# Seven block products in place of eight in part of a fused attention and feed-forward kernel

## The chip, the cores and the metric

The kernel runs on one core of a Trainium2 chip. Its engines are named as the profile names them: PE (TensorE, matmuls; its weight loads are PEld), DVE (VectorE), ACT (ScalarE), POOL (GpSimd) and SP (SyncE, which here only issues DMAs). The metric is the device time in microseconds, as the median of several runs; lower is better.

## The reference

A linear attention makes `x`, and a multiplicative feed-forward is applied to it:

```
q_s = exp(q - max_d(q));  q_s /= sum_d(q_s) + 1e-9          # q, k, v: 8 batches x 8 heads x 576 x 64, float32
k_s = exp(k - max_s(k));  k_s /= sum_s(k_s) + 1e-9
x   = q_s @ (k_s^T @ v)          # per batch and head; laid out as 4608 tokens x 512
h   = (x @ w1) * (x @ w2) @ w3   # w1, w2: 512 x 1024;  w3: 1024 x 1024
out = h @ w_out                  # w_out: 1024 x 512;  out: 4608 x 512, float32
```

## The kernel before

`w3 @ w_out` is multiplied out first (`fold`, lines 337 to 350: transposes `w3t`, their copies `w3T`, products `pf`, and the scaled copy `W3O`, kept in 16 bits). What is left per token group is two "up" products, `x @ w1` and `x @ w2`, their product `ab`, and one "down" product `ab @ W3O`.

There are nine token groups `c`. Groups 0 to 7 hold 512 tokens of one batch each; group 8 (`xtail`) holds the 64 tokens per batch that are left over. `attention(b)` makes the group's `x`: column maxima of k (`kmx`, `cb`), subtraction and exponential (`ksub`, `kexp`), a 16-bit copy of v (`vc`), the small products `kv`, and for q the row maximum, subtraction, exponential, sum and normalisation (`qmx`, `qsub`, `qexp`, `qsm`, `qeps`, `qrc`, `qn`), a transposing DMA (`qd`), and the products `xm` and `xt` with their copies `xs` and `xts`, which write `x`.

`chunk(c)` holds the feed-forward of a group. The 1024 hidden columns are worked in slices of 128 (lines 716 to 748). For one slice `up(…, 1)` accumulates four matmuls (the 512 inputs in blocks of 128) of `x @ w2` over 512 tokens in one PSUM bank; `bs` copies that bank to SBUF in 16 bits; `up(…, 0)` does the same with `w1`; `ab` multiplies the second bank by the copy (line 741, always on DVE). Groups 0 and 1 are cut into two halves of 256 tokens, so that their matmuls have 256 columns; all others have 512. `down(tb)` accumulates eight matmuls of 512 output columns for 128 tokens; `os` copies the bank and `store` sends it off from SP. In group 8 the last block of 128 tokens is cut into three parts (`down2`, `os2`, `tail`).

All work is put into a `Plan` as steps with an engine, their inputs (`needs`) and what they take and give back: PSUM banks (`ps`, eight), output buffers (`osb`, six), the 16-bit copies (`bsb`, six). A text, `ORDER`, lists the steps one by one. A letter after a slash chooses the engine where there is a choice (A for ACT, D for DVE, P for POOL). Each engine works through its own steps in just this order, and waits only for the inputs and buffers of the step that is next. Steps marked `port` that lie on POOL and DVE are linked in `run`: where two of them follow each other on different engines, the later one waits for the earlier one. Steps on ACT, and DVE steps without the mark (`ab`, `bs`, `os`, reductions), are not linked.

## Time and profile before

| what | value |
|---|---|
| median of 3 runs | 235.95 us (235.83 to 236.02) |
| profiled execution, span from the first to the last instruction | 234.6 us |
| granted PE clock | 1.000 |
| PE busy | 228.0 us, 1938 matmuls |
| DVE busy | 185.7 us, 310 instructions |
| ACT busy | 112.8 us, 178 instructions |
| POOL busy | 115.7 us, 77 instructions |
| DMA | 46.84 MB, mean 200 GB/s |

The profile gives the profiled execution's span; the runs are some 1.35 us longer than that, for what lies before the first and behind the last instruction. In rows of groups, a line holds the source line, the engine, the operation, output and inputs with their shapes, the count, then busy time in us and the mean duration of one in ns, then the idle time of the engine just before, and what ended it. In rows of a time line or of the chain of waits the first number is the start in us from the start of the span, the second the length in us. "128x512" is 128 partitions of 512 elements.

### The profile page before, as it was taken

How to read it: one execution, taken by the hardware profiler on the slowest of the kernel's cores; microseconds unless marked ns; L12 is line 12 of the kernel's file. 1: busy time of each engine (PE TensorE's matmuls, PEld its weight loads, DVE VectorE, ACT ScalarE, POOL GpSimd, SP SyncE). 2: the span in 40 equal slices, each digit the busy share in tenths (PEclk: the TensorE clock that was granted, in tenths of full speed). 3: DMA queues.
4: the chain of work that ended last, by engine and by line, in shares of the span. 5: the costliest groups of instructions: out<-in, count | busy, mean ns of one | idle time of the engine just before them, and what ended most of it. 6: DMA issues, size and time to landing. Idle time of an engine off the chain costs nothing.

```text
span 234.6 us, 4828 instructions
## 1 busy us (share of the span) xinstructions
PE 228.0 (97%) x1938; PEld 119.6 (51%) x1938; DVE 185.7 (79%) x310; ACT 112.8 (48%) x178; POOL 115.7 (49%) x77
## 2 busy tenths in 40 slices
PE   7898999999999999999999999999999999999995
PEld 2454568856876445444444444444544444444443
DVE  3989779989999999999899979979686247634642
ACT  2646763686737876675885265344504210000101
POOL 8244410788969399799938983790700000000000
DMA  6999999999999996999499997453391016005035
GB/s 221 215 293 224 305 243 243 389 274 276 273 298 334 398 373 187 252 402 332 42 218 396 268 236 229 91 25 79 70 183 30 0 36 145 0 6 129 3 75 193
DMA packets 38358, 46.84 MB, mean 200 GB/s; under 512 B 18368, under 2 KB 21824, under 8 KB 38336
## 3 DMA queue, kind: packets, MB, share of 16 engines
q1 hardware_dynamic: 32464, 35.92, 55.6%
q0 software_dynamic: 5728, 10.55, 19.2%
q8 instruction: 15, 0.25, 0.4%
q10 hardware_dynamic: 144, 0.07, 0.1%
q14 instruction: 7, 0.06, 0.1%
HBM read 38.80 MB, written 9.44 MB: 206 GB/s over the span
## 4 chain that ended last, share of the span: by engine, by line
PE 89%; DMA 9%; POOL 1%; issue 0%; ACT 0%; POOLq 0%
PE pab L726 53%; PE po L748 24%; DMA w<-in_moe_w_dram 9%; PE pf L347 3%; PE po L763 3%; PE pkv L443 2%; PE xm L582 2%; PE w3t L337 1%; PE xt L582 1%; POOL w L305 0%; PE pkv L452 0%; POOL ident masks.py:199 0%; ACT osb L223 0%; POOL ident masks.py:197 0%; POOLq masks.py:199 0%
## 5 line engine op out<-in xcount | busy, mean ns | idle before, releaser
L726 PE MATMUL pab<-x,w2sb 128*128 128x512 f16 (+1 forms) x320 | 64.9, 337 | 0.0
L726 PE MATMUL pab<-x,w1sb 128*128 128x512 f16 (+1 forms) x320 | 64.9, 337 | 0.0
L741 DVE TENSOR_TENSOR ab<-pab,bsb 128x512 f16<-128x512 f32 x72 | 47.7, 682 | 16.8 <-PE pab L726 15.2
L748 PE MATMUL po<-W3O,ab 128*128 128x512 f16 x256 | 58.4, 379 | 0.0
L223 ACT CAST bsb<-pab 128x512 f16<-128x512 f32 x49 | 28.0, 584 | 49.5 <-PE pab L726 49.3
L726 PEld LDWEIGHTS <-w1sb 128*128 128x128 f16 x352 | 34.3, 98 | 27.7
L726 PEld LDWEIGHTS <-w2sb 128*128 128x128 f16 x352 | 34.1, 98 | 28.1 <-issue 0.2
L417 POOL TENSOR_TENSOR k<-k,cb 128x1152 f32<-128x1152 f32 x13 | 34.0, 2628 | 19.2 <-DVE q L486 10.3
L748 PEld LDWEIGHTS <-ab 128*128 128x128 f16 x256 | 24.4, 98 | 30.0 <-issue 2.3
L530 POOL TENSOR_TENSOR en<-eq,qr 128x1024 f16<-128x1024 f16 (+1 forms) x14 | 29.6, 2125 | 16.7 <-ACT qr L518 10.5
L378 DVE TENSOR_REDUCE km<-k 128x128 f32<-128x1152 f32 x14 | 30.3, 2167 | 0.0
L223 ACT COPY osb<-po 128x512 f32<-128x512 f32 (+2 forms) x26 | 14.7, 564 | 28.7 <-PE po L748 17.6
L486 POOL TENSOR_TENSOR q<-q,qm 128x1280 f32<-128x1280 f32 (+1 forms) x13 | 27.8, 2144 | 0.9 <-DVE qm L480 0.9
L480 DVE TENSOR_REDUCE qm<-q 128x16 f32<-128x1024 f32 (+2 forms) x16 | 21.2, 1331 | 3.8 <-DMA q<-in_q_dram 3.8
L494 ACT ACTIVATE eq<-q 128x1024 f16<-128x1024 f32 (+2 forms) x16 | 18.7, 1169 | 9.4 <-DVE q L486 8.5
L512 DVE TENSOR_REDUCE qr<-eq 128x16 f32<-128x1024 f16 (+2 forms) x16 | 21.3, 1340 | 0.2 <-ACT eq L494 0.2
L425 ACT ACTIVATE ek<-k 128x1152 f16<-128x1152 f32 x16 | 18.1, 1161 | 6.2 <-POOL k L417 6.2
L223 DVE CAST bsb<-pab 128x512 f16<-128x512 f32 x23 | 15.8, 687 | 6.4 <-PE pab L726 6.1
L227 ACT ACTIVATE x<-xm 128x512 f16<-128x512 f32 x27 | 14.4, 600 | 12.5 <-PE xm L582 12.5
L347 PE MATMUL pf<-wosb,w3T 128*128 128x512 f16 x64 | 15.6, 379 | 0.4 <-DMA wosb<-in_moe_w_out_dram 0.4
L223 DVE COPY osb<-po 128x512 f32<-128x512 f32 (+1 forms) x12 | 7.8, 654 | 9.0 <-PE po L748 4.6
L223 ACT COPY w3T<-w3t 128x1024 f16<-128x1024 f16 x8 | 8.1, 1011 | 5.3 <-PE w3t L337 4.1
(64 smaller groups left out, 175.4 us busy)
## 6 DMA issues: line engine op xcount, KB each, us to landing
out_dram<-osb SPq DMA_DIRECT2D x65, 128.0 KB, 3.1
q<-in_q_dram SPq DMA_DIRECT2D x6, 1152.0 KB, 8.4
k<-in_k_dram SPq DMA_DIRECT2D x6, 1152.0 KB, 6.9
v<-in_v_dram SPq DMA_DIRECT2D x6, 1152.0 KB, 8.7
w<-in_moe_w_dram POOLq DMA_DIRECT2D x8, 256.0 KB, 11.6
q<-in_q_dram SPq DMA_DIRECT2D x2, 576.0 KB, 4.3
k<-in_k_dram POOLq DMA_DIRECT2D x2, 576.0 KB, 13.4
k<-in_k_dram POOLq DMA_DIRECT2D x1, 1152.0 KB, 14.4
```

The costliest lines, as they stand in the source:

```text
L223: return [(nc.scalar.copy if eng == "ACT" else engine[eng].tensor_copy)(out=out, in_=in_)]
L347: nc.tensor.matmul(st["pf", ft], lhsT=st["w3T", ft][:, gt, :], rhs=wosb[:, gt, :], start=(gt == 0), stop=(gt == N_FT - 1))
L378: dve.tensor_reduce(out=st["km", b][:, two(hp), :], in_=kb[:, two(hp), :, :].rearrange("p h j d -> p h d j"), axis=AX.X, op=ALU.max)
L417: return [engine[eng].tensor_tensor(out=kb[:, two(hp), :, :], in0=kb[:, two(hp), :, :], in1=st["cb", b][:, two(hp), None, :].broadcast_to( ...
L480: dve.tensor_reduce(out=st["qm", b][:, hs, j], in_=qb[:, hs, j, :], axis=AX.X, op=ALU.max, **({"negate": True} if (b, p) in FEXP else {}))
L486: return [engine[eng].tensor_tensor(out=qb[:, hs, j, :], in0=qb[:, hs, j, :], in1=st["qm", b][:, hs, j, None].broadcast_to([P, nh, n, D]), ...
L494: nc.scalar.activation(out=st["eq", b, p], in_=qb[:, hs, j, :], func=AF.Exp)
L512: dve.tensor_reduce(out=st["qr", b][(slice(None), *part(p))], in_=st["eq", b, p], axis=AX.X, op=ALU.add)
L530: return [engine[eng].tensor_tensor(out=st["en", b][:, j, hs, :].rearrange("p j h d -> p h j d"), in0=st["eq", b, p], in1=st["qr", b][:, h ...
L726: nc.tensor.matmul(st["p", one, c, sub, u][:, a * (t1 - t0):(a + 1) * (t1 - t0)], lhsT=w[:, ct, fb * P:(fb + 1) * P], rhs=x()[:, ct, t0:t1 ...
L741: dve.tensor_tensor(out=st["ab", c][:, nf * u:nf * u + nf, t0:t1], in0=cut(st["p", 0, c, sub, u]), in1=cut(st["bsb", c, sub, u]), op=ALU.mult)
L748: nc.tensor.matmul(st["po", c, tb], lhsT=st["ab", c][:, ft, tb * P:(tb + 1) * P], rhs=W3O[:, ft, :], start=(ft == 0), stop=(ft == N_FT - 1))
```

## The change

In the last three groups (`SU`: 6, 7 and 8) the up products, and in groups 5, 6 and 7 (`SD`) the down products, are computed as 2 x 2 blocks by Winograd's form of Strassen's algorithm: seven block products, with sums and differences of blocks before and after, in place of eight.

For the up products the blocks of one factor are the upper and lower half (of the 512 inputs) of `w1` and of `w2`; those of the other are the two halves of the inputs and the two halves of 256 tokens of `x`. The result's four blocks are `x @ w1` and `x @ w2` for the two token halves. One set of seven products is made for each `g`, a slice of 256 hidden columns, of which a group has four. A block product `um` is four matmuls of 256 columns (two slices of 128 hidden columns, two blocks of 128 inputs) into one bank. Products 1, 6, 5 and 3 follow each other in the same bank A, each added to what is there; products 7 and 4 share bank B; product 2 has bank C. Between them copies `ue` leave the banks as float32 into eight scratch slots (`sc`, the parts of the first input buffers of q and v): of 1, of 1+6, of 1+6+5, and of 7. Sums `uc` then give `x @ w1` of the first half (1: DVE, from bank C), `x @ w2` of the first half (3: DVE, from bank B) and of the second half (4: POOL or DVE, from two scratch slots). `ab` of the first half is a product of two SBUF operands (POOL or DVE), that of the second half reads bank A (DVE).

Sums ahead of the products: `ws`, eight steps of 1024 elements once, for `w1` and `w2` (seven on POOL, one on DVE, in the place of `w316`), and `xd`, four steps of 512 elements for each of the three groups (eight on DVE, four on POOL). For the down products `wt` makes four differences of `W3O` blocks once (1024 elements, all on POOL), `ad` four sums of `ab` blocks per group (1024 elements, nine on DVE, three on POOL); `dm` is a block product of eight matmuls of 256 columns, in banks A, B and C as above, with copies `de`, sums `dc` and two stores of twice 256 KB per group in place of four of 256 KB.

Counted over the whole: 48 `up` steps with 24 `bs` and 24 `ab`, and 12 `down` steps with 12 `os`, become 84 `um`, 48 `ue`, 36 `uc`, 24 `ab`, 12 `xd`, 8 `ws`, 21 `dm`, 12 `de`, 12 `dc`, 12 `ad` and 4 `wt`. PSUM keeps eight banks and there are still six output buffers, now in one tile (`outs`); the transposed `w3T` and a buffer of `kmx` move into the tile `aux` that `wt` later writes.

`ORDER` is the same up to the second group's third up product (`up.1.1.0.2`), and written anew from there on. The weight sums lie on POOL between `qsub.2.1` and `ksub.7.0`, except `ws.4.1`, on DVE in the last stage. Four `vc` steps more are on ACT instead of POOL. Of the 48 `bs` steps that remain 44 are on ACT and 4 on DVE (before: 49 and 23); of the `os` steps 22 are on ACT and 4 on DVE (before: 26 and 12). The attention of the last group ends later, among the block products, and the stores `st.0.0` and `st.0.1` leave after the group 4 products have begun.

The diff, cut; the part of `ORDER` that is shown runs from the end of group 5's up products to the last store:

```diff
--- before.py
+++ after.py
...
+    def own(self, ring, aps):
+        self.slots[ring] = list(aps)
+
+    def grab(self, s):
+        free = self.slots[s["takes"]]
+        got = [free.pop(0) for _ in range(s["slots"])]
+        self.held[s["name"]] = sorted(k for k, _ in got), got[0][1], s["takes"]
+
+    def free(self, name):
+        ks, _, ring = self.held.pop(name)
+        self.slots[ring] += [(k, self.full[ring][k]) for k in ks]
...
+ksub.7.1/P qd.6.0 xm.6.0 qsm.7.1 xm.6.1 xs.6.1.1/A xt.5 xts.5.1/D st.4.0 down.4.2 xs.6.0.0/A st.4.1 xs.6.0.1/D
+xd.6.1/P um.6.0.1 os.4.2/D xs.6.1.0/A xd.6.2/D xt.6 xts.6.1/A um.6.1.1 ue.6.1.1/A up.1.5.0.7 um.6.1.2 xts.6.0/D
+ue.6.0.1/D st.3.3 um.6.0.6 vc.7.0/A ab.5.0.6 bs.5.0.7/A xd.6.3/D um.6.1.6 ue.6.1.2/A xts.5.0/A um.6.0.7 ad.5.3/D
+qeps.7.1/A ue.6.0.7/A qsm.7.0 um.6.1.7 up.0.5.0.7 xd.6.4/D uc.6.1.1 dm.5.1 ue.6.0.2/D ue.6.1.7/A qrc.7.1 qeps.7.0/A
+qrc.7.0 kexp.7.1 ab.5.0.7 down.4.3 ad.5.1/D ad.5.2/D de.5.1/A um.6.1.4 uc.6.1.3 os.4.3/A um.6.0.2 qn.7.1/P um.6.0.4
+uc.6.0.3 um.6.0.5 um.6.2.1 uc.6.0.1 ue.6.0.4/D uc.6.0.4/D st.3.2 um.6.2.7 um.6.3.1 dm.5.2 ue.6.3.1/A ws.4.1/D qn.7.0/D
+ue.6.2.1/A um.6.2.2 st.3.0 dc.5.1 uc.6.2.1 um.6.1.5 dm.5.6 ue.6.1.4/A um.6.0.3 ab.6.0.1 de.5.2/A uc.6.1.4/P um.6.3.6
+qd.7.0 um.6.2.6 um.6.1.3 ab.6.1.1 dm.5.7 de.5.7/D ue.6.2.7/A um.6.2.4 qd.7.1 dm.5.5 ue.6.2.2/A uc.6.2.3 ad.5.4/P
+kexp.7.0 ab.6.1.0/P kv.7 kv2.7 dm.5.4 ue.6.3.2/A um.6.3.5 um.6.2.5 xm.7.0 xm.7.1 ab.6.2.0/P de.5.4/A dc.5.3 xs.7.0.1/D
+xs.7.1.1/D st.4.2 dc.5.4/P ue.6.2.4/A uc.6.2.4/D xs.7.0.0/A xd.7.1/D xs.7.1.0/A xd.7.3/D dm.5.3 dc.5.2/A um.6.3.2
+uc.6.3.1 xd.7.2/D xt.7 xts.7.1/A st.5.1 um.6.3.7 ue.6.3.7/A ue.6.3.4/A um.7.0.1 ue.7.0.1/A ab.6.0.0/D ad.6.3/D
+um.6.2.3 um.7.2.1 xts.7.0/D ab.6.2.1 st.5.0 xd.8.1/D um.7.1.1 ue.7.1.1/A um.7.0.7 xd.7.4/D ue.7.0.7/A um.7.0.6
+ue.7.0.2/A um.6.3.4 uc.6.3.3 um.6.3.3 uc.6.3.4/P um.7.1.7 ue.7.1.7/D um.7.0.5 um.7.0.4 ue.7.0.4/A uc.7.0.4/P ab.6.3.1
+dm.6.7 uc.7.0.3 um.7.0.2 ue.7.2.1/A uc.7.0.1 ab.7.0.0/P um.7.0.3 ab.7.0.1 um.7.1.6 ue.7.1.2/A um.7.1.4 uc.7.1.3 dm.6.1
+de.6.1/A um.7.1.5 ue.7.1.4/A ad.6.1/D ad.6.2/D ab.6.3.0/D ad.6.4/D um.7.2.7 um.7.1.2 uc.7.1.1 uc.7.1.4/P um.7.3.2
+um.7.3.1 ue.7.3.1/A uc.7.3.1 dm.6.6 de.6.2/A um.7.2.6 um.7.3.6 ue.7.2.2/A xd.8.3/P ue.7.2.7/A ue.7.3.2/A dm.6.2 dc.6.1
+um.7.2.2 uc.7.2.1 um.7.2.5 ue.7.2.4/A um.7.2.4 uc.7.2.3 um.7.3.7 ue.7.3.7/D um.8.0.1 um.7.1.3 ab.7.1.0/P xd.8.2/P
+de.6.7/A ab.7.1.1 uc.7.2.4/D dm.6.4 um.7.3.4 um.7.2.3 uc.7.3.3 dm.6.5 de.6.4/A um.8.0.2 xd.8.4/P dc.6.3 ab.7.2.0/D
+dc.6.4/P ue.8.0.1/D uc.8.0.1 ab.7.3.0/D um.8.0.7 ue.8.0.7/A um.7.3.5 ue.7.3.4/D uc.7.3.4/P um.8.1.1 ue.8.1.1/A dm.6.3
+um.8.1.7 ue.8.1.7/A ad.7.3/P um.8.1.6 um.8.2.1 ue.8.1.2/A ab.7.2.1 ue.8.2.1/A um.7.3.3 ab.7.3.1 um.8.1.4 um.8.1.2
+uc.8.1.3 st.4.3 um.8.1.5 um.8.0.6 ue.8.1.4/D uc.8.1.4/P ue.8.0.2/A um.8.2.6 uc.8.1.1 ab.8.1.0/P dc.6.2/D st.6.0
+um.8.0.4 ue.8.2.2/A um.8.2.2 uc.8.2.1 um.8.3.1 um.8.0.5 ue.8.0.4/A uc.8.0.4/P dm.7.1 um.8.3.7 de.7.1/A uc.8.0.3
+ab.8.0.0/P um.8.2.7 um.8.2.5 ue.8.3.1/D um.8.3.6 um.8.3.2 ue.8.3.7/D ue.8.2.4/A ue.8.3.2/D um.8.3.4 uc.8.3.3 um.8.2.3
+um.8.3.5 uc.8.3.1 um.8.0.3 ad.7.1/P ad.7.2/D ue.8.2.7/A um.8.2.4 st.6.1 uc.8.2.3 dm.7.7 de.7.7/D ab.8.2.0/D dm.7.6
+dm.7.2 dc.7.1 dm.7.4 uc.8.2.4/D ab.8.2.1 ab.8.3.0/D de.7.2/A dc.7.3 dm.7.5 down.8.0 os.8.0/A st.8.0 de.7.4/D
+ue.8.3.4/A um.8.1.3 ab.8.1.1 dc.7.4/P ab.8.0.1 uc.8.3.4/D down.8.1 os.8.1/A st.7.1 st.8.1 ad.7.4/D um.8.3.3 ab.8.3.1
+down.8.2 os.8.2/A st.8.2 dm.7.3 down.8.3.0 down.8.3.256 dc.7.2/A os.8.3.256/D down.8.3 st.7.0 os.8.3.0/D st.8.3.256
+st.8.3.0 os.8.3/A st.8.3
...
+    SU = [6, 7, 8]
+    SD = [5, 6, 7]
+    flat = lambda t: t.rearrange("p h j d -> p (h j d)")
+    auxf = flat(aux)
+    w3Tbuf = [auxf[:, i * 1024:(i + 1) * 1024].rearrange("p (r c) -> p r c", r=N_FT) for i in range(2)]
+    kmtbuf = auxf.bitcast(F32)[:, 1024:2048].rearrange("p (h j d) -> p h j d", h=HH, j=4)
+    wsum = w316.rearrange("p (s k) f -> p s k f", s=4)
+    turn = lambda c, cs: (c - min(cs, default=0)) % 2
+    adbuf = [flat(t).bitcast(F16)[:, 0:4096].rearrange("p (s f t) -> p s f t", s=4, f=4) for t in inbuf["k"]]
+    xdbuf = [t.rearrange("p a j i d -> p (a j i d)")[:, 0:2048].rearrange("p (s k t) -> p s k t", s=4, k=2)
+             for t in v16buf]
+    plan.own("osb", [(i, outs[:, i, :]) for i in range(6)])
+    spare = [flat(inbuf[n][i])[:, 512 * x:512 * x + 512] for i in range(1) for n in "qv" for x in range(4)]
+    plan.own("sc", list(enumerate(spare)))
+    plan.own("w3T", list(enumerate(w3Tbuf)))
...
+        def xd(i, eng):
+            X, xv = xdbuf[turn(c, SU)], x()
+            lo, hi = slice(0, 256), slice(256, 512)
+            a, b = {1: (xv[:, 0:2, hi], xv[:, 0:2, lo]), 2: (xv[:, 2:4, hi], X[:, 0]),
+                    3: (xv[:, 2:4, hi], xv[:, 0:2, hi]), 4: (xv[:, 2:4, lo], X[:, 1])}[i]
+            return minus(eng, X[:, i - 1], a, b)
+
+        BANK = {1: "A", 6: "A", 5: "A", 3: "A", 7: "B", 4: "B", 2: "C"}
+
+        def um(g, p):
+            X, xv = xdbuf[turn(c, SU)], x()
+            lo, hi = slice(0, 256), slice(256, 512)
+            w, k0, r = {1: (w1sb, 0, xv[:, 0:2, lo]), 2: (w1sb, 2, xv[:, 2:4, lo]), 3: (wsum[:, 3], 0, xv[:, 2:4, hi]),
+                        4: (w2sb, 2, X[:, 3]), 5: (wsum[:, 0], 0, X[:, 0]), 6: (wsum[:, 1], 0, X[:, 1]),
+                        7: (wsum[:, 2], 0, X[:, 2])}[p]
+            t = bank2(("u" + BANK[p], c, g))
+            for u in range(2):
+                fb = 2 * g + u
+                for kk in range(2):
+                    nc.tensor.matmul(t[:, u, :], lhsT=w[:, k0 + kk, fb * P:(fb + 1) * P], rhs=r[:, kk, :],
+                                     start=(p in (1, 2, 7) and u == 0 and kk == 0), stop=(u == 1 and kk == 1),
+                                     skip_group_check=True)
+
+        def slot(name):
+            return plan.held[name][1].rearrange("p (u t) -> p u t", u=2)
+
+        def ue(g, k, eng):
+            t = st["u" + BANK[{1: 1, 2: 6, 4: 5, 7: 7}[k]], c, g]
+            st["us", c, g, k] = slot(("ue", c, g, k))
+            return copy(eng, st["us", c, g, k], t)
+
+        def uc(g, k, eng):
+            s = lambda i: st["us", c, g, i]
+            if k == 1:
+                return minus(eng, s(1), st["uC", c, g], s(1), ALU.add)
+            st["ub", c, g, k] = work.tile([P, 2, 256], F16, tag="bsb", name="bsb", bufs=6)
+            return minus(eng, st["ub", c, g, k], *((st["uB", c, g], s(2)) if k == 3 else (s(4), s(7))), ALU.add)
+
+        def abp(g, h, eng):
+            if ("ab", c) not in st:
+                st["ab", c] = work.tile([P, N_FT, 512], F16, tag="ab", name="ab")
+            a, b = (st["uA", c, g] if h else st["us", c, g, 1]), st["ub", c, g, 3 + h]
+            return minus(eng, st["ab", c][:, 2 * g:2 * g + 2, 256 * h:256 * h + 256], a, b, ALU.mult)
...
+        def ad(i, eng):
+            Y, ab = adbuf[turn(c, SD)], st["ab", c]
+            q4 = lambda r, s: ab[:, 4 * s:4 * s + 4, 256 * r:256 * r + 256]
+            a, b = {1: (q4(1, 0), q4(1, 1)), 2: (Y[:, 0], q4(0, 0)), 3: (q4(0, 0), q4(1, 0)), 4: (q4(0, 1), Y[:, 1])}[i]
+            return minus(eng, Y[:, i - 1], a, b, ALU.add if i == 1 else ALU.subtract)
...
+            t = bank2(("d" + BANK[p], c))
+            for i in range(2):
+                for f in range(4):
+                    nc.tensor.matmul(t[:, i, :], lhsT=l[:, f, i * P:(i + 1) * P], rhs=r[:, f, :],
+                                     start=(p in (1, 2, 7) and i == 0 and f == 0), stop=(i == 1 and f == 3),
+                                     skip_group_check=True)
...
+            o = st["do", c, r][:, :, (0 if k in (1, 3) else 256):(256 if k in (1, 3) else 512)]
+            if k == 2:
+                return copy(eng, o, st["dA", c])
+            return minus(eng, o, st["dC" if k == 1 else "dB", c] if k < 4 else s(4), s({1: 1, 3: 2, 4: 7}[k]), ALU.add)
+
+        def store2(r):
+            for i in range(2):
+                if c < B:
+                    to = out[c * S:(c + 1) * S, :].rearrange("(p j) c -> p j c", j=NJ)[:, 4 * r + i:4 * r + i + 3:2, :]
+                    nc.sync.dma_start(out=to, in_=st["do", c, r][i * HALF:(i + 1) * HALF, :, :])
...
+                U(1, xn[0] + [("w1", i) for i in range(len(CUTS["w1"]))], takes="ps")
+                U(7, [("xd", c, 3)] + wsn(3), takes="ps")
+                U(2, xn[1], takes="ps")
+                E(1, [n("um", 1)] + sc0)
+                E(7, [n("um", 7)] + sc0, gives=[])
+                Cc(1, [n("um", 2), n("ue", 1)], "DVE", gives=[n("um", 2)])
+                U(6, [n("ue", 1), ("xd", c, 2)] + wsn(2))
+                E(2, [n("um", 6)] + sc0)
+                U(4, [n("ue", 7), ("xd", c, 4)])
+                Cc(3, [n("um", 4), n("ue", 2)], "DVE", takes="bsb", gives=[n("um", 7), n("ue", 2)])
+                U(5, [n("ue", 2), ("xd", c, 1)] + wsn(1))
+                E(4, [n("um", 5)] + sc0)
+                Cc(4, [n("ue", 4), n("ue", 7)], PAIRS, takes="bsb", gives=[n("ue", 4), n("ue", 7)], port=True)
+                U(3, [n("ue", 4)] + wsn(4))
+                A(("ab", c, g, 0), PAIRS, lambda eng, g=g: abp(g, 0, eng), [n("uc", 1), n("uc", 3)] + old,
+                  gives=[n("ue", 1), n("uc", 3)], port=True, kind="abp")
+                A(("ab", c, g, 1), "DVE", lambda g=g: abp(g, 1, "DVE"), [n("um", 3), n("uc", 4)] + old,
+                  gives=[n("um", 1), n("uc", 4)], kind="abm")
...
+    def ws(s, kk, eng):
+        a = lambda r, h: (w1sb, w2sb)[r][:, 2 * h + kk, :]
+        x, y = {1: (a(1, 0), a(1, 1)), 2: (wsum[:, 0, kk], a(0, 0)), 3: (a(0, 0), a(1, 0)),
+                4: (a(0, 1), wsum[:, 1, kk])}[s]
+        return [engine[eng].tensor_tensor(out=wsum[:, s - 1, kk], in0=x, in1=y,
+                                          op=ALU.add if s == 1 else ALU.subtract)]
+
+    def wt(i, eng):
+        o4 = lambda r, s: W3O[:, 4 * r:4 * r + 4, 256 * s:256 * s + 256]
+        x, y = {1: (o4(0, 1), o4(0, 0)), 2: (o4(1, 1), aux[:, 0]), 3: (o4(1, 1), o4(0, 1)), 4: (o4(1, 0), aux[:, 1])}[i]
+        return [engine[eng].tensor_tensor(out=aux[:, i - 1], in0=x, in1=y, op=ALU.subtract)]
```

238 lines of the change are left out of this document (164 added, 74 removed).

## The prediction

> **What bounds the kernel now.** I read the page's head first, then the chain of waits in order of time, then busy time by stretches, and only then groups and single instructions.
>
> ```profile
> span 234.6 us, 4828 instructions
> PE 228.0 (97%) x1938; PEld 119.6 (51%) x1938; DVE 185.7 (79%) x310; ACT 112.8 (48%) x178; POOL 115.7 (49%) x77
> ```
>
> The chain of waits (start us, us, what, matmuls):
>
> ```profile
> 33.81 13.97 PE pab L726 x128
> ...
> 55.98 5.24 PE pab L726 x48
> ...
> 61.62 7.09 PE pab L726 x64
> ...
> 124.25 13.81 PE pab L726 x64
> 138.06 5.18 PE po L748 x24
> ...
> 209.22 13.81 PE pab L726 x64
> 223.03 1.73 PE po L748 x8
> 224.75 6.96 PE po L763 x48
> 231.72 0.02 issue
> 231.74 0.27 ACT osb L223
> ```
>
> Busy time in three stretches: the middle, the last third, the tail. Clock and DMA share stand behind POOL:
>
> ```profile
> core 0: us, PE busy (x) PEld busy (x) DVE busy (x) ACT busy (x) POOL busy (x), PEclk, DMA share, GB/s
> 56.00:157.00 101.00, 101.00 (x939) 52.43 (x937) 95.95 (x164) 64.43 (x106) 82.52 (x42) 1.00 0.88 255
> 157.00:224.70 67.70, 67.70 (x416) 30.79 (x415) 40.98 (x69) 13.70 (x23) 6.05 (x3) 1.00 0.34 61
> 224.70:234.60 9.90, 7.00 (x49) 3.90 (x46) 2.37 (x4) 1.22 (x3) 0.00 (x0) 1.00 0.54 159
> ```
>
> The reader is to see three things. From 33.81 us the chain is TensorE alone, back to back, to a last copy at 231.74. TensorE is busy in all of the 101.00 and the 67.70 us at granted clock 1.00, so it doesn't wait. In the middle VectorE (95.95 of 101.00) and GpSimd (82.52) are nearly full; in the last stretch VectorE has 26.7 us free, ScalarE 54, GpSimd 61.6. So a matmul taken away shortens the run by its spacing, so long as the added element-wise work fits into that room.
>
> The page gives 234.6 us for the profiled span. The three runs have a median of 235.95, so 1.35 us lie around the span; I carry them over unchanged. Differences below about 0.2% (0.5 us) can't be told from no change here.
>
> **What is removed from TensorE.** A 512-column matmul takes 13.81/64 = 0.2158 us (up) and 5.18/24 = 0.2158 (down). A 256-column one takes 13.97/128 = 0.1091 in the first group, or 7.09/64 = 0.1108 in the second.
>
> - Up, three groups: 64 matmuls of 512 become 4 slices x 7 products x 4 = 112 of 256. 13.81 - 112 x 0.1091 = 1.59 us each, 4.77 us together.
> - Down, three groups: 32 of 512 (6.91 us) become 7 x 8 = 56 of 256 (6.11 us). 0.80 us each, 2.39 us together.
>
> Sum 7.1 us. With 0.1108 it is 3 x (1.40 + 0.70) = 6.3 us. I take 7.1, since 128 matmuls carry the lower spacing. Everything before the second group's third product stands in the old order, so the start doesn't move.
>
> **What is added, by rows.** These groups price the new operations (mean ns of one is the number behind the bar's comma):
>
> ```profile
> L741 DVE TENSOR_TENSOR ab<-pab,bsb 128x512 f16<-128x512 f32 x72 | 47.7, 682 | 16.8 <-PE pab L726 15.2 <-ACT bsb L223 1.1
> L726 PEld LDWEIGHTS <-w1sb 128*128 128x128 f16 x352 | 34.3, 98 | 27.7
> L417 POOL TENSOR_TENSOR k<-k,cb 128x1152 f32<-128x1152 f32 x13 | 34.0, 2628 | 19.2 <-DVE q L486 10.3 <-DVE cb L413 5.1 <-issue 2.7
> L486 POOL TENSOR_TENSOR q<-q,qm 128x1280 f32<-128x1280 f32 x7 | 16.4, 2343 | 0.0
> L530 POOL TENSOR_TENSOR en<-eq,qr 128x1280 f16<-128x1280 f16 x7 | 16.4, 2340 | 12.8 <-ACT qr L518 7.0 <-DMA out_dram<-osb 4.8 <-DVE qr L523 0.7
> L223 ACT COPY osb<-po 128x512 f32<-128x512 f32 x24 | 14.0, 585 | 24.4 <-PE po L748 17.6 <-PE po L763 5.5 <-DMA v<-in_v_dram 1.1
> L530 POOL TENSOR_TENSOR en<-eq,qr 128x1024 f16<-128x1024 f16 x7 | 13.4, 1910 | 3.9 <-ACT qr L518 3.6 <-DVE qr L523 0.3
> L486 POOL TENSOR_TENSOR q<-q,qm 128x1024 f32<-128x1024 f32 x6 | 11.5, 1911 | 0.9 <-DVE qm L480 0.9
> L223 POOL CAST v<-v 128x1152 f16<-128x1152 f32 x9 | 10.2, 1148 | 0.6 <-PE xm L582 0.4 <-DMA v<-in_v_dram 0.2
> L223 DVE COPY osb<-po 128x512 f32<-128x512 f32 x11 | 7.6, 686 | 8.4 <-PE po L748 4.6 <-DMA out_dram<-osb 2.8 <-PE po L763 1.0
> L385 DVE TENSOR_TENSOR kmx<-k 128x1024 f32<-128x1024 f32 x1 | 1.2, 1214 | 0.0
> L393 DVE TENSOR_TENSOR kmx<-kmx 128x512 f32<-128x512 f32 x1 | 0.7, 693 | 0.0
> L223 DVE COPY qT<-qtp 128x512 f16<-128x512 f16 x1 | 0.4, 362 | 0.0
> ```
>
> And single instructions: back-to-back rates, and how long a result takes to reach the next engine:
>
> ```profile
> 17.18 1.01 ACT L223 COPY w3T<-w3t 128x1024 f16<-128x1024 f16 x1 [0.33 <-PE w3t L337]
> ...
> 18.29 1.03 PE L347 MATMUL pf<-wosb,w3T 128*128 128x512 f16 x4
> ...
> 56.14 2.34 POOL L486 TENSOR_TENSOR q<-q,qm 128x1280 f32<-128x1280 f32 x1
> ...
> 110.91 2.45 DVE L741 TENSOR_TENSOR ab<-pab,bsb 128x512 f16<-128x512 f32 x4
> ...
> 165.81 4.20 POOL L530 TENSOR_TENSOR en<-eq,qr 128x1280 f16<-128x1280 f16 x2 [6.96 <-ACT qr L518]
> ...
> 202.15 1.03 PE L726 MATMUL pab<-x,w2sb 128*128 128x512 f16 x4
> 203.01 1.03 PE L726 MATMUL pab<-x,w1sb 128*128 128x512 f16 x4
> 203.21 0.58 ACT L223 CAST bsb<-pab 128x512 f16<-128x512 f32 x1 [11.50 <-PE pab L726]
> ```
>
> *Weight loads.* Each 256-column matmul has its own load, 98 ns, under a 109 ns spacing: hidden, as in the two groups that already run so. Cost 0; uncovered it would show as spacing, which 0.1108 bounds.
>
> *The last stage,* from the first block product to the end. TensorE's list is 84 up products x 0.436 + 21 down products x 0.873 + 8.7 of plain down products + 3.3 of other work = 67.0 us. The new order gives VectorE 100 instructions there. 75 are of 512 elements with f32 or PSUM operands: 0.69 alone, but (2.45 - 0.69)/3 = 0.59 in a row, say 0.60: 45 to 52 us. Eight 512-element and ten 1024-element differences are all 16-bit; no row has such an operation. From above the f32 rows bound them (0.69 and 1.21: 17.6 us), from below the 16-bit copy (0.36 and 0.72: 10.1 us). Seven others make 4.5 us. Sum 60 to 74 us against 67.0. I take 62, near the lower end, because work in a row goes at 0.60 and the 16-bit copy is the only row of that width. VectorE then fits with 5 us to spare. ScalarE has 65 instructions of at most 0.585 us (38 us); GpSimd 23, 27 to 31 us: both fit.
>
> *Round trips in one bank.* A slice's products 1, 6, 5 and 3 add up in one PSUM bank, and a copy must leave between each two. In the rows above the w2sb product has been issued at 203.01, ScalarE starts at 203.21 and takes 0.58; a ScalarE result that is ready at 17.18 + 1.01 = 18.19 is used by TensorE at 18.29. A trip takes 0.20 + 0.58 + 0.10 = 0.88 us (0.99 through VectorE). The order has at least three other products, 1.31 us, in between everywhere. So each trip is hidden if its copy starts within 0.3 to 0.4 us, less than one further operation in front. ScalarE is idle half the time; but the copy may also wait for one of eight scratch slots, which a VectorE or GpSimd sum gives back. Behind a late copy the whole TensorE queue stands. Bounds: 0, and 60 trips (12 slices and 3 down groups, four each) x 0.2 = 12 us. I take 1.0, five times a delay of 0.2.
>
> *The middle, GpSimd.* Eleven sums of weights (1024 elements, 16-bit) join its queue, and four casts (1.15 each) leave it for ScalarE. From the end of the instruction at 56.14 (58.48) to the first difference of x that group 6 needs, the queue holds 12 ksub x 2.63, ten qsub and ten qn (half 1.91, half 2.34), 4 casts x 1.15 and 11 weight sums: 31.5 + 42.5 + 4.6 + 11 x 1.91 = 99.6 us, and a difference of 512 elements, 1.0. Two in a row gain 0.05 (4.20 against 4.25), some 2 us over 49. It ends at 157 to 159 without any idle time. TensorE reaches product 6 of the first slice at 159.6 (55.98, where the second group starts, + 103.0 us of matmuls that the new order puts in between, at the spacings above, + 0.6, since the same count over the old order comes out 1 us short in 176), and a VectorE difference and handoff of 0.7 must come first: 158.9. So GpSimd goes from 82% to full. If the weight sums ran at the k row's rate (2628/1152 = 2.28 ns an element, 2.33 each) they would add 4.7 us, and TensorE would wait 3 to 5 us. The bounds are 0 and 5; the en row, 16-bit too, is the nearest (1.91). I take 0.5.
>
> [...]
>
> [...]
>
> *Order and stores.* Loads keep their bytes; four stores of the first groups go out later, behind loads. Nothing reads them but their output slots, of which there are still six. Cost 0; if a slot comes late a copy waits, and behind it a bank. At the end, a 512 KB store of group 7 leaves SP just ahead of the last ones. A usual one:
>
> ```profile
> out_dram<-osb SPq DMA_DIRECT2D x65, 128.0 KB, 3.1
> ```
>
> Its last copy ends 1.77 - 0.78 = 1.0 us before TensorE does; 3.1 us from there against 2.9 us of tail now (234.6 - 231.7). Bounds 0 and 1; I take 0.3.
>
> **Sum.** 234.6 - 7.1 + 1.0 + 0.5 + 0.3 = 229.3 span, + 1.35 = 230.6 us, 2.3% faster.
>
> **Rivals.**
> 1. *GpSimd late* (chance 0.15). The weight sums at 2.33 us push the attention of the later groups: 3 more than the sum, 233.5. For it: the queue is full by my count, and any wait for VectorE comes on top. Against: the en row.
> 2. *VectorE becomes the bound of the last stage* (0.09). At 74 us, no overlap and 16-bit at the f32 rate, TensorE waits 74 - 67 = 7 us: 230.6 - 1.0 + 7 = 236.6, slower. It decides from 73 us on, 6 over TensorE's list. Against: the row of four in 2.45.
> 3. *Missed round trips* (0.09). Copies stand behind one more operation (0.6 - 0.35 = 0.25 late) in most of 60 trips, and the delay passes into the next: at 0.2 each, 12 us instead of 1, 241. It decides from 0.12 us a trip (7.1/60). Against: ScalarE's idle half. For: VectorE feeds the same banks and frees the slots.
> 4. *The products don't run faster* (0.02): the 256-column spacing rises to 0.2158 x 64/112 = 0.123 us, and nothing is gained: 236 to 237. Both 256-column rows are against it.
>
> The forecast has 0.65: 228.6 to 232.5 is its own range. Half of rivals 2 and 4 lies within 0.2% or below; so faster 0.83, same 0.03, slower 0.14. The range over all, 228.5 to 235.5, starts just under 235.95 - 7.1, where nothing is lost, and leaves out the slower cases.
>
> **What would show it.** Right: the chain from 34 us still TensorE, 112 block matmuls per group at 0.109, VectorE near 62 us busy or under 72 in the last stage, and small TensorE waits there. Wrong in rival 1: TensorE waits between 100 and 160 us for GpSimd or for products of the attention. Rival 2: VectorE over 95% busy after 157 us and in the chain. Rival 3: many waits of 0.2 to 1 us of TensorE for ScalarE copies. The prediction fails if these waits together pass 6 us.

## The result, and the profile after

The changed kernel takes 239.06 us (238.59 to 239.82), the kernel before, run beside it, 235.99 (235.83 to 236.46): a ratio of 1.0127, interval 1.0106 to 1.0149. So it is 1.3% slower; 230.6 us was forecast.

Head of the page of the changed kernel, and its busy time in the middle, in the block products and behind the last product:

```profile
span 237.1 us, 5390 instructions
...
PE 223.1 (94%) x2154; PEld 140.8 (59%) x2154; DVE 203.7 (86%) x344; ACT 137.9 (58%) x223; POOL 162.3 (68%) x106
...
core 0: us, PE busy (x) PEld busy (x) DVE busy (x) ACT busy (x) POOL busy (x), PEclk, DMA share, GB/s
56.00:163.00 107.00, 102.62 (x955) 53.01 (x953) 98.02 (x167) 69.79 (x113) 103.32 (x50) 1.00 0.85 243
163.00:231.20 68.20, 68.13 (x665) 55.47 (x663) 59.47 (x104) 34.49 (x63) 32.20 (x24) 1.00 0.29 70
231.20:237.10 5.90, 0.00 (x0) 0.00 (x0) 0.19 (x1) 0.27 (x1) 0.00 (x0) 0.74 0.52 141
```

TensorE is busy 4.9 us less than before (223.1 against 228.0). But in the middle, where it was never idle, it now waits 107.00 - 102.62 = 4.38 us. And the end, from the last product on, has grown from 2.9 to 5.9 us. Among the block products TensorE is busy without a break, 68.13 of 68.20 us, and they follow each other as closely as was forecast: eight matmuls of 256 columns every 0.87 us, 0.109 each.

```profile
165.46 1.04 PE L866 MATMUL uA<-v,w 128*128 128x256 f16 x8
166.33 1.04 PE L866 MATMUL uB<-v,w 128*128 128x256 f16 x8
```

What TensorE waits for in the middle (us in all, times, longest):

```profile
PE xm L626 <- DMA qT<-en: 2.1, 2, 1.8
PE pab L782 <- DVE ab L797: 1.9, 1, 1.9
```

The first is a transposing DMA of the second group: 1.8 us, from 61.8. The second is a product `ab`, from 128.7 us. TensorE's and VectorE's time lines there:

```profile
127.66 1.03 PE L782 MATMUL pab<-x,w1sb 128*128 128x512 f16 x4
130.60 0.59 PE L782 MATMUL pab<-x,w2sb 128*128 128x512 f16 x2 [1.92 <-DVE ab L797]
```

```profile
117.98 2.19 DVE L422 TENSOR_REDUCE km<-k 128x128 f32<-128x1152 f32 x1
120.08 1.22 DVE L524 TENSOR_REDUCE qm<-q 128x16 f32<-128x1024 f32 x1
...
124.26 4.30 DVE L422 TENSOR_REDUCE km<-k 128x128 f32<-128x1152 f32 x2 [0.79 <-DMA k<-in_k_dram]
128.46 1.49 DVE L524 TENSOR_REDUCE qm<-q 128x20 f32<-128x1280 f32 x1
129.85 0.70 DVE L797 TENSOR_TENSOR ab<-pab,bsb 128x512 f16<-128x512 f32 x1
```

Between the `ab` that starts at 117.39 and the one at 129.85 VectorE works, but for some small steps, only on maxima for later groups. A bank is given back by its `ab`, so TensorE runs out of banks and stops.

The profile's wait is a little shorter than what is lost. Four matmuls of 512 columns that follow each other are due every 0.86 us (4 x 0.2158), but show as busy for 1.03. So TensorE could have gone on at 128.52, and went on at 130.60: 2.08 us. A wait under 0.17 us doesn't show at all. By the starts of the matmuls there are five waits over 0.2 us in the middle, 5.2 us together, where the profile shows 4.4.

The stores at the end, on SP's and ScalarE's queues of the changed kernel, and the time the smallest takes from issue to landing, before and after:

```profile
225.96 1.25 SPq L930 DMA_DIRECT2D out_dram<-outs  x2
227.30 2.26 SPq L812 DMA_DIRECT2D out_dram<-outs  x2
230.06 1.51 SPq L930 DMA_DIRECT2D out_dram<-outs  x2
231.62 0.40 ACTq L812 DMA_DIRECT2D out_dram<-outs  x1
231.66 1.31 SPq L812 DMA_DIRECT2D out_dram<-outs  x2
```

```profile
out_dram<-osb ACTq DMA_DIRECT2D x1, 64.0 KB, 1.6
```

```profile
out_dram<-outs ACTq DMA_DIRECT2D x1, 64.0 KB, 4.0
```

Two times 512 KB (line 930, group 7) stand among the stores of group 8, and 64 KB need 4.0 us in place of 1.6.

### The profile page after: what moved, and what is told of

Same layout as the page of the kernel before. It is cut to its first block, busy times and chain, and to the rows that moved or that the text cites. A ratio compares the mean times of both kernels' runs of the same rounds, so it can differ in the third digit from the quotient of the medians.

```text
span 237.1 us, 5390 instructions
## 1 busy us (share of the span) xinstructions
PE 223.1 (94%) x2154; PEld 140.8 (59%) x2154; DVE 203.7 (86%) x344; ACT 137.9 (58%) x223; POOL 162.3 (68%) x106
## 4 chain that ended last, share of the span: by engine, by line
PE 47%; DMA 17%; POOL 16%; DVE 7%; issue 7%; ACT 2%; SPq 1%; POOLq 1%; DVEq 0%; ACTq 0%
PE pab L782 20%; PE po L804 8%; PE uA L866 5%; DMA w<-in_moe_w_dram 5%; DMA wosb<-in_moe_w_out_dram 4%; POOL en L574 4%; DVE km L422 3%; DMA qT<-en 3%; DMA k<-in_k_dram 3%; PE pf L391 3%; PE uB L866 2%; POOL k L461 2%; PE dA L906 2%; POOL q L530 2%; DMA out_dram<-outs 2%
## 5 line engine op out<-in xcount | busy, mean ns | idle before, releaser
L782 PE MATMUL pab<-x,w2sb 128*128 128x256 f16 (+1 forms) x256 | 48.5, 326 | 1.9 <-DVE ab L797 1.9
L782 PE MATMUL pab<-x,w1sb 128*128 128x256 f16 (+1 forms) x256 | 48.5, 326 | 0.0
L461 POOL TENSOR_TENSOR k<-k,cb 128x1152 f32<-128x1152 f32 x13 | 34.0, 2629 | 10.2 <-DVE q L530 10.2
L804 PE MATMUL po<-W3O,ab 128*128 128x512 f16 x160 | 37.4, 380 | 0.0
L782 PEld LDWEIGHTS <-w1sb 128*128 128x128 f16 x256 | 24.7, 98 | 16.2 <-issue 0.4
L574 POOL TENSOR_TENSOR en<-eq,qr 128x1280 f16<-128x1280 f16 (+1 forms) x13 | 27.7, 2142 | 9.3 <-DVE k L845 7.8
L797 DVE TENSOR_TENSOR ab<-pab,bsb 128x512 f16<-128x512 f32 x48 | 31.4, 678 | 1.8 <-ACT bsb L267 1.2
L267 ACT COPY outs<-po 128x512 f32<-128x512 f32 (+1 forms) x22 | 12.5, 578 | 15.2 <-PE po L819 6.5
L866 PEld LDWEIGHTS <-w 128*128 128x128 f16 x192 | 18.7, 98 | 2.8
L391 PE MATMUL pf<-wosb,aux 128*128 128x512 f16 x64 | 15.6, 379 | 0.5 <-DMA wosb<-in_moe_w_out_dram 0.5
L866 PE MATMUL uA<-v,w 128*128 128x256 f16 x96 | 13.3, 273 | 0.0
```

The costliest lines, as they stand in the source:

```text
L267: return [(nc.scalar.copy if eng == "ACT" else engine[eng].tensor_copy)(out=out, in_=in_)]
L391: nc.tensor.matmul(st["pf", ft], lhsT=st["w3T", ft][:, gt, :], rhs=wosb[:, gt, :], start=(gt == 0), stop=(gt == N_FT - 1))
L461: return [engine[eng].tensor_tensor(out=kb[:, two(hp), :, :], in0=kb[:, two(hp), :, :], in1=st["cb", b][:, two(hp), None, :].broadcast_to( ...
L574: return [engine[eng].tensor_tensor(out=st["en", b][:, j, hs, :].rearrange("p j h d -> p h j d"), in0=st["eq", b, p], in1=st["qr", b][:, h ...
L782: nc.tensor.matmul(st["p", one, c, sub, u][:, a * (t1 - t0):(a + 1) * (t1 - t0)], lhsT=w[:, ct, fb * P:(fb + 1) * P], rhs=x()[:, ct, t0:t1 ...
L797: dve.tensor_tensor(out=st["ab", c][:, nf * u:nf * u + nf, t0:t1], in0=cut(st["p", 0, c, sub, u]), in1=cut(st["bsb", c, sub, u]), op=ALU.mult)
```

## The experiments

Four questions, in the order in which they came up. Each edit is to the changed kernel unless another is named; in `ORDER` only the moved steps are shown. Most variants of the changed kernel scatter by 1 to 2 us from run to run, some by 3 and more, the kernel before by 0.6 to 1.2, so differences under 1 us between two variants count for little. Of the changed kernel's four runs the longest, 239.82 us, has the lowest mean granted clock, 0.986, and the shortest, 238.59, has 1.000.

### Is GpSimd too full? (e1_light)

```diff
-    out=wsum[:, s - 1, kk], in0=x, in1=y
+    out=wsum[:, s - 1, kk, 0:64], in0=x[:, 0:64], in1=y[:, 0:64]
-    out=aux[:, i - 1], in0=x, in1=y
+    out=aux[:, i - 1, :, 0:16], in0=x[:, :, 0:16], in1=y[:, :, 0:16]
```

> The changed kernel, with the weight sums cut to a sixteenth of their columns (and four of the seven down block products reading plain blocks of W3O in place of the sums): the result is not the reference's. GpSimd loses about ten times 2 us, some 20 us, between 58 and 157 us; nothing else changes. Theory 1, GpSimd is too full in the middle: the 1.9 us wait of TensorE for the DVE product ab at 128.7 us goes, the first up block product (163.2 us in the changed kernel) starts 2 to 3 us earlier, 236 to 237 us in all; the 1.8 us wait for a transposed q at 61.8 us stays, since the first weight sum comes only at 58.8. Rival, the two waits come from the order of the transfers on SP or from full DMA engines alone: both waits stay and the time stays within 0.5 of 239.0.

Measured: 238.25 us, 0.8 less than the changed kernel. The middle of this run:

```profile
56.00:161.80 105.80, 101.94 (x949) 52.49 (x947) 97.35 (x166) 69.37 (x113) 83.01 (x49) 1.00 0.84 243
```

GpSimd is back at the 83 us that it had before, and TensorE still waits 3.9 us: 1.9 at the first wait, 1.4 of 1.9 at the second. So GpSimd's extra work costs some 0.8 us, no more than the scatter. The theory that I began with, rival 1's, falls: the chain of waits does run through GpSimd's queue from 93 to 114 us, but VectorE and the transfers are right behind it.

### Which order costs what in the middle? (e2_q3, e3_k6, g1_ab)

```diff
 e2_q3:  -q.3 cb.2 qd.1.1 k.3        +cb.2 qd.1.1 k.3 q.3
 e3_k6:  -qd.4.0 .. qd.4.1 .. k.6    +k.6 qd.4.0 .. qd.4.1
 g1_ab:  -kmx.6.0 .. qmx.6.1 .. ab.4.0.0 .. ab.4.0.1
         +ab.4.0.0 kmx.6.0 .. ab.4.0.1 qmx.6.1
```

> The changed kernel with one load moved: q of group 3 leaves SP behind the transposing DMA of the second group and the k load, as in the kernel before, and not ahead of both. If that load's traffic is what makes the transposing DMA take 7 us, it takes 5 us again, the 1.8 us wait of TensorE at 61.8 us goes, and the time is 237.2 if nothing later takes the gain back. Rival, GpSimd is the bound of the middle: the gain at 62 us is given back by the later wait at 128.7 us, which grows from 1.9 to some 3.5 us, and the time stays within 0.5 of 239.0.

> The changed kernel with one load moved: k of group 6 leaves SP ahead of the two transposing DMAs of group 4, which wait for GpSimd's normalised q until 114 us. Theory, it is the place on SP: the load leaves at 110 to 112 in place of 116.9 us, the maxima of k on VectorE no longer stand in front of the product ab, the wait of 1.9 us at 128.7 goes, 237.2 in all. Rival 1, GpSimd's full queue sets the pace: the next product that needs GpSimd is late in its place, and no more than 0.7 us is gained. Rival 2, the load is slow because the DMA engines are full: it leaves earlier, takes longer, and gains less than 1 us.

> The changed kernel with two steps moved on VectorE: the products ab.4.0.0 and ab.4.0.1 stand ahead of kmx.6.0 and of qmx.6.1. In the changed kernel VectorE is busy without a gap from 115.07 to 130.55 (but 0.79 us) and works 12 us of column maxima between two products, while TensorE has work for 11. Theory, VectorE's order is the cause of the 1.9 us wait at 128.7: the wait goes, 237.2 in all, or a little less gain where VectorE is next late with something else. Rival, GpSimd's or the transfers' lateness behind it: another wait of 1.5 us or more follows before the first up block product, which starts at 162.7 or later (163.2 in the changed kernel); time within 0.5 of 239.0.

Measured: 240.47, 237.59 and 237.92 us. With q.3 behind, the wait at 62 us goes, but a `q` maximum then waits 1.6 us for its load, TensorE waits 0.8 us for VectorE, up to 68.6, and 1.8 us for the next transposing DMA, up to 77.5: the wait moved and grew. The later wait for `ab` grows too, to 2.3 us, and the matmuls behind it take up to 1.91 us in place of 1.03 (shown in the last section), some 1.7 us more. With k.6 in front, the wait at 128.7 goes and one of 2.0 us for a transposed q comes, up to 121.8; 1.5 us are gained. With `ab` in front of the maxima the 1.9 us wait for `ab` goes for good (0.7 us of small ones take its place) and 1.1 us are gained. So the wait at 128.7 was VectorE's order, with the late load of k.6 in it (VectorE waits 0.79 us for it in the time line above); the other one, as far as e2_q3 shows, is a queue of transfers in which whatever stands second is late.

### Does the old order of the middle give it back? (h1_old, h2_old_tail, i1_old, i4_old_plain7, j1_old_early, j2_old_early_tail, k1_old_sums, k2_old_sums_tail, l1_light_dve)

The middle up to `qd.6.1` in the order of the kernel before, the rest in the changed order, the sums of weights set into gaps:

```diff
+ORDER of before, up to qd.6.1, with
+  h1: W3O.2/A wt.1/P wt.3/P wt.2/P        i1: wt.1/P wt.3/P wt.2/P ksub.1.0/P
+  qn.2.1/P ws.1.0/P   vc.3.0/P ws.1.1/P   ksub.5.0/P ws.3.0/P   wt.4/P ws.3.1/P qn.6.1/P
+  qd.6.1 ws.2.0/P ws.2.1/D
+then the steps that are left, in the changed order
```

> The changed kernel with the middle in the order of the kernel before, up to the transposing DMAs of group 6, and the rest in the changed order. The twelve sums of weights stay: three of wt on GpSimd in its idle 8 us before 42, four of the rest in its gaps before 145, two later, and two on VectorE; none of them takes part in the linking of POOL and DVE. Theory, the new order of the middle (VectorE's maxima ahead of products, loads ahead of transposing DMAs) is what costs 5 us: no TensorE wait between 56 and 157, first up block product at 157 to 159 in place of 163.2, 233.0 to 235.0. Rival, GpSimd's extra 20 us are the cause: waits of 3 us or more come back in the middle or before the first block products, and the time is over 236.

> The changed kernel with the middle in the order of the kernel before, up to the transposing DMAs of group 6, and the rest in the changed order; the twelve sums of weights stay, three of them now behind the last load that GpSimd issues (in the run before they stood ahead of four loads of weights and held TensorE up for 10 us). Theory, the new order of the middle is what costs 5 us: no TensorE wait between 56 and 155, first up block product at 158 to 160 in place of 163.2, 234 to 236. In the run before, the first block products waited some 6 us for x of group 6, which is made closer to its use in this order; if that comes back, some 2 to 4 us of the gain go and the time is 236 to 238. Rival, GpSimd's extra 20 us are the cause: waits of 3 us or more between 56 and 155.

h1_old took 254.89 us: the three `wt` stood ahead of DMAs that GpSimd issues, a load of w1 came late, and TensorE waited 10.0 us, from 37. i1_old mends that: 243.66 us. Its middle, and the 15 us behind it:

```profile
56.00:159.60 103.60, 103.12 (x947) 53.19 (x944) 96.85 (x164) 64.54 (x106) 94.76 (x47) 1.00 0.88 255
159.60:175.00 15.40, 10.68 (x70) 6.30 (x70) 10.38 (x16) 8.23 (x16) 6.21 (x4) 0.67 0.15 28
```

With the old order the middle has 0.5 us of waits, though seven of the sums are in it and GpSimd is at 94.76: once more not GpSimd. But x of group 6, in the old order, is made just in time for products that came later than the block products do. TensorE waits 4.7 us in all, most of them for it, and the granted clock is 0.67 on the mean of these 15.40 us: 0.50 for some 10.2 us.

j1_old_early makes q of group 6 earlier (`qsm.6.0`, `qn.6.0`, `qd.6` ahead of group 7's maxima); k1_old_sums moves two sums and three more steps (`qsm.7.1`, `kexp.7.1`, `vc.7.1`) out of the way besides:

```diff
 j1: -kmx.7.0 cb.7 qsm.6.0 qeps.6.0/A   +qsm.6.0 qeps.6.0/A kmx.7.0 qrc.6.0 cb.7
     -ksub.7.0/P vc.7.0/P qn.6.0/P      +qn.6.0/P qd.6.0 ksub.7.0/P vc.7.0/P
     ws.2.0/D ws.2.1/D behind ab.5.0.5; xd.6.1/D; up.1.5.0.7 behind xt.5
 k1: ws.2.0/D ws.2.1/D behind kmx.7.0; qsm.7.1 behind ue.6.0.1/D
```

> The middle in the order of the kernel before, as in the run before last, with q of group 6 made earlier: qsm.6.0, qeps.6.0 and qrc.6.0 ahead of the maxima of k of group 7, qn.6.0 ahead of ksub.7.0, its transposing DMA right behind; kexp.7.1 and vc.7.1 behind the copies that TensorE waits for; four of the sums of weights and xd.6.1 on VectorE; up.1.5.0.7 ahead of the first block product. Theory, the order of the middle costs 4 to 5 us and nothing else: no TensorE wait over 1 us between 56 us and the end, clock 1.00 throughout, last product at 226.5 to 228 in place of 231.2, 234.0 to 235.5. Rival, the gain is lost at the first block products: waits of 2 us or more between 155 and 175, and 236.5 or more.

> The run with the old middle and the early q of group 6, with the two sums ws.2 moved from in front of the copies of x to a place at 150 us where VectorE waits and GpSimd is idle, qsm.7.1 behind the first copies of the block products, and kexp.7.1 and vc.7.1 behind theirs. Theory: the 3.3 us wait goes, and with it the half clock behind it (some 2.6 us more); no TensorE wait over 1 us anywhere after 56 us; last product at 228 to 229 in place of 234.1; 233.5 to 235.2, just under the kernel before. Rival, the block products' start waits for the next thing on VectorE or ScalarE: 236 or more.

Measured: 239.89 and 238.24 us. k1_old_sums, middle, first block products, rest:

```profile
56.00:160.00 104.00, 103.97 (x965) 53.86 (x963) 97.69 (x167) 65.95 (x109) 94.23 (x47) 1.00 0.90 258
160.00:176.00 16.00, 12.58 (x106) 9.17 (x104) 14.69 (x27) 9.50 (x19) 3.39 (x2) 1.00 0.00 1
176.00:231.50 55.50, 55.00 (x551) 45.14 (x551) 47.16 (x82) 25.84 (x47) 28.98 (x22) 1.00 0.32 78
```

In the middle TensorE doesn't wait, 103.97 of 104.00 us. Then 3.4 us are lost in 16, nearly all in waits for VectorE, which is at 14.69 of 16.00, and the last product ends at 231.5: where it ended in the changed kernel. The two largest:

```profile
165.22 1.05 PE L866 MATMUL uB<-v,w 128*128 128x256 f16 x8 [1.29 <-DVE v L845]
172.19 0.60 PE L866 MATMUL uA<-x,w1sb 128*128 128x256 f16 x4 [1.37 <-DVE bsb L845]
```

The last run takes VectorE's work away just there:

```diff
 l1, on k1: -in_=st["eq", b, p]          +in_=st["eq", b, p][:, :, :, 0:D if b < 7 else 4]
            -out=wsum[:, s - 1, kk]      +out=wsum[:, s - 1, kk, 0:n]     # n = 64 for ws.4
```

> The run before (old middle, no waits there) with part of VectorE's work among the first block products left out: the two sums of q of group 7 (qsm.7.1 and qsm.7.0, 1.48 and 1.21 us) add 4 of 64 columns, and the sums of weights ws.4 (0.64 each) carry a sixteenth of their columns, so that group 7's and other block products' results are not the reference's. Some 3.5 us of VectorE go between 162 and 176 us. Theory, VectorE's work there is what takes the middle's gain: TensorE's waits between 160 and 176 fall from 4.3 to under 1.5 us, the last product ends at 228 to 229 in place of 231.5, 234.8 to 236.0 in all. Rival, the round trips or the copies on ScalarE: the waits stay above 3 us and the time above 237.5.

```profile
160.00:176.00 16.00, 13.96 (x119) 10.63 (x118) 13.50 (x29) 9.75 (x19) 4.22 (x3) 1.00 0.00 1
```

Measured: 236.60 us, over the range expected. TensorE's loss there falls from 3.4 to 2.0 us, and the last product ends 1.9 us earlier, at 229.6. Of the two waits above the first is gone: that much is VectorE's work. The second, 1.37 us for a VectorE sum, is as long as it was, with VectorE's work cut. In this run VectorE itself stands idle ahead of that sum, 1.88 us up to 168.34, in the row of a reciprocal that waits for ScalarE. So this second wait is one of order, not of too much work on VectorE.

Four runs combined this with changes of the end. 

> Both: the middle in the order of before and the new end. If the two losses are independent, 231.0 to 232.5, the forecast's sum. If the end is bound by the transfers that the middle leaves over (the middle in the old order has the stores of the first groups done earlier), the gain at the end is the same or larger; if the earlier arrival only moves the wait to the last stage, it is over 234.

 

> Both: the middle in the order of before and group 7's down products plain. If the losses in the middle and at the end are independent: the time of the first of these four runs less 2 us, 232 to 234, under the kernel before. If the middle's gain is lost at the first block products, 235 to 236.

 

> The same with the new end of the second study (dm.7.3 and its store earlier, two stores from ScalarE's queue). That end gained little by itself, and the end is bound by some 2 MB of stores at 180 GB/s: 0.3 to 1.0 us under the run before.

 

> The same with the new end of the second study, which cost 1.5 us with the old middle in the run before, though its own stretch was not longer: 0 to 1.0 us under the other of these two if that was scatter, over it by 1 us or more if the end itself is worse.

 They took 254.44, 245.39, 241.36 and 239.13 us, far over what was expected of them (h2_old_tail has h1_old's late load): none gained a microsecond over its partner (h1, i1, j1 and k1 in this order), three were 0.9 to 1.7 us slower, and why is not settled.

### What makes the end long? (e4_tail, g2_tail, i2_cut7, i3_plain7, j3_small)

```diff
 e4, g2: dm.7.3, dc.7.2/A, st.7.0 ahead of the last block products of group 8
 g2:     -OWN = (3, 384)   +OWN = [(1, 0), (2, 0), (3, 384)]     # stores from ScalarE's queue
 i2:     -nc.sync.dma_start(out=to, ..[i * HALF:(i + 1) * HALF, :, :])
         +nc.sync.dma_start(out=to[:, :, 0:w], ..[.., :, 0:w])   # w = 32 for group 7
 i3:     -SD = [5, 6, 7]   +SD = [5, 6]                          # down.7.0 to 3 spread over group 8
```

> The changed kernel with the end reordered: the last down block product of group 7 (dm.7.3), the sums before it, its output copy and its 512 KB store stand ahead of the last up block products and the third block of group 8, some 3 us earlier. Theory, the small last stores land behind the 512 KB of group 7: the time from the last product to the end falls from 5.8 to 3 to 3.5 us, and the time to 236.3 to 236.8. Rival, the tail has another cause (the number of stores on SP, the clock): it stays above 5 us and the time within 0.5 of 239.0.

> The changed kernel with a new end: the sum ad.7.4 ahead of dc.7.3, the copy de.7.4 on ScalarE, the block product dm.7.3, its copy and its 512 KB store three steps earlier; the stores of the second and third block of group 8 leave from ScalarE's queue, and the copies of blocks 2 to 4 of group 8 take free scratch slots instead of output slots. Theory, what makes the end long is that 2 MB of stores leave SP in the last 12 us, in issues of 0.6 us each, with the last small ones behind the 512 KB of group 7: the end comes 3 to 3.5 us after the last product in place of 5.8, 236.4 to 236.9. Rival, the stores are bound by the transfers themselves: the end stays above 5 us and the time within 0.5 of 239.0.

> The changed kernel in which the four stores of group 7 carry 32 of their 512 columns: the rest of that group's output is not written. The issues stay, 0.94 MB of 2 MB in the last 12 us go. Theory, the end is bound by the transfers, which move some 180 GB/s there: the time from the last product to the end falls from 5.8 to 2.5 to 3.5 us, the last small store lands in 1.6 to 2.2 us in place of 4, and the time is 236 to 236.8. Rival, the issues or the small stores' own latency: the end stays above 5 us.

> The changed kernel with block products in the down products of groups 5 and 6 alone: group 7's four down products are plain again, spread over the up block products of group 8, three of them 4 to 14 us before the place of the old ones, and the stores of 256 KB go as each is done. TensorE's list grows by 0.8 us. Theory, stores too late and too close together are the cause of the long end: it falls from 5.8 to 3 us or less, and the time to 237 at most. Rival, the block products of group 8 need the down block products as filler: TensorE waits 2 us or more in the last 20 us, and nothing is gained.

e4_tail took 239.95 us, its four times from 238.15 to 241.95, and decides nothing. g2_tail took 239.06: its end is 5.5 us in place of 5.9, although its last issue on SP ends 1.0 us behind the last product in place of 1.8; so the issues are not the main cause. i2_cut7 took 236.31 us, with an end of 3.5 us and

```profile
out_dram<-outs ACTq DMA_DIRECT2D x1, 64.0 KB, 1.6
```

So the bytes of group 7's stores are the cause: 2 MB go out from 224.9 to 237.1, 0.17 MB per us, and the 64 KB of ScalarE's queue, issued at 231.62, take 4.0 us to land, 1.6 without those bytes. i3_plain7 took 238.36 us: its end is 3.3 us, but TensorE needs 70.8 us in place of 68.2 for the block stage (0.8 for the plain products, 1.8 in waits), and what the end gained is gone.

j3_small joins g1_ab, e3_k6 and g2_tail: 

> The changed kernel with its own order of the middle and three of the single edits together: ab.4.0.0 and ab.4.0.1 ahead of the maxima, the load of k of group 6 ahead of the transposing DMAs, and the new end. Alone they gave 1.1, 1.5 and 0 to 1 us. If the first two act on the same wait at 128.7 us they do not add: 237.0 to 237.6. If they are independent: 235.5 to 236.5.

 238.20 us (237.19 to 240.27): they don't add up, since two of them act on one wait, and the wait for the transposed q that e3_k6 brought stays (1.8 us, up to 122.1).

No version beat the kernel before, not even those that leave work out (i2_cut7 236.31 us, l1_light_dve 236.60).

## Why the prediction was wrong

The forecast was 230.6 us, the profiled run took 238.87. The difference, by its steps: the middle 5.9 us (product 6 of the first slice at 165.5 in place of 159.6), the end 2.7, the time around the span 0.4, less 0.8 us in the block stage. Two steps failed: the order of the middle, put at "Cost 0", and the tail store, put at 0.3.

- **What is removed from TensorE** (7.1): right. The spacing of 0.109 is there, and the block stage, from product 6 of the first slice to the last product, was to take 66.5 us (159.6 to 226.1) and took 65.7 (165.5 to 231.2). TensorE's busy time fell by 4.9 us only; most of the difference to 7.1 is short waits, and 0.17 us of each longer one, that count as busy.
- **Weight loads, round trips, VectorE in the last stage**: right. TensorE is idle 0.07 us there, and by the starts of the matmuls some 0.5 us late in all, where 1.0 was taken for trips. VectorE is busy 59.5 us, where I took 62. The 16-bit differences of two full operands, which no row had shown:

```profile
L845 DVE TENSOR_TENSOR v<-x,v 128x512 f16<-128x512 f16 x4 | 1.7, 417 | 0.0
L845 DVE TENSOR_TENSOR k<-ab 128x1024 f16<-128x1024 f16 x4 | 2.8, 690 | 0.1
L1062 POOL TENSOR_TENSOR w<-w2sb 128x1024 f16<-128x1024 f16 x2 | 4.3, 2129 | 0.0
```

  On VectorE they take 0.42 and 0.69 us, where the f32 rows take 0.69 and 1.21, so they are some 1.7 times as fast. Rivals 2, 3 and 4 didn't come.
- **The middle, GpSimd** (0.5): its size was about right, 0.8 by e1_light, but that was luck. The wait was to come at product 6 of the first slice, where TensorE doesn't wait; what e1_light gains lies within the scatter, and the wait that became shorter by it is the one for `ab`. A sum takes 2.13 us, not 1.91, which is 2.4 us more over eleven; no wait of TensorE for GpSimd came of it, and rival 1 didn't come. It named the place (TensorE waiting between 100 and 160 us) with the wrong engine.
- **Order and stores, in the middle** ("Cost 0"): this step failed. I compared bytes and engines, not where steps stand on SP's and VectorE's queues. A load (q.3) ahead of a transposing DMA, and 12 us of maxima between two `ab`, are the two large waits; all waits of the middle come to 4.4 us by the profile, 5.2 by the starts of the matmuls. With `ab` ahead of the maxima (g1_ab) 1.1 us came back, and with the old order (k1_old_sums) the middle had no wait. The window that I quoted had the warning: VectorE 95.95 of 101.00. I used GpSimd's number from that row and not VectorE's.
- That it is more than this one order, k1_old_sums makes likely: without any wait in the middle the same time is lost at the first block products. From 56 us to the last product VectorE has 157 to 160 us of work and TensorE 171, in 175. I summed VectorE for the last stage alone, where it fits; in the first 16 us of it, with the attention of group 7 still to do, it is nearly full. But a nearly full VectorE alone makes no wait: in the changed kernel it is busy 12.63 of the 13.00 us from 163 to 176, and TensorE doesn't wait there. l1_light_dve shows 1.4 of the 3.4 us to be VectorE's work; the rest is order again. i1, j1 and k1 show that taking one wait away brings up the next. Whether some order loses less than 4 us stays open.
- **The tail store** (bounds 0 and 1, 0.3 taken): failed; the end grew by 3.0. I followed the landing of one store of group 7 against TensorE's end, by the row of a 128 KB piece, though this store goes in two of 256 KB. What counts is how many bytes are left: the block form finishes a group's four output blocks together, so that group 7's 1 MB meets group 8's. It costs 2.4 us (5.9 against 3.5 without those bytes).

With the two failed steps at 4.4 in place of 0 and 3.0 in place of 0.3 the sum gives 237.8; of the 1.1 us that are left to 238.87, 0.8 are the part of the waits that counts as busy.

## What to carry to other kernels

Where a trace shows two engines near full in one stretch, sum both by stretches before taking work from one: here the saving went only as far as the other engine's order let it, and a wait removed from one place turned up where that engine was next behind (k1_old_sums: 0.03 us of waits in the middle, 3.4 in the 16 us behind it). A chain of waits that runs through an engine doesn't price it; cutting that engine's work and finding the time nearly unchanged does (e1_light: 20 us less on GpSimd, 0.8 us less in all). A form that finishes outputs in larger pieces and later moves stores to the end, where in this case what was left to send decided the time (5.9 us, and 3.5 with 0.94 MB less) and no longer the size of the last store.
